# A Fourier-mixing layer with a one-token FFN: FFN weights in 128-row groups, and one ordered load list over remapped slots

## The chip, the cores and the metric

The kernel runs on one core of a Trainium2 chip. The metric is the device time of one execution in microseconds (us). Several executions were timed, and one more was profiled; all trace rows come from that one.

## The reference

A layer of 2048 tokens and 512 features with adaptive layer norm in front of two parts. `c` is one vector; six rows of 512 come from it.

```python
mod = (_silu(c) @ w_mod).reshape(1, 6, 1, -1)
sa, ca, ga, sb, cb, gb = (mod[:, i] for i in range(6))
h = _layernorm(x) * (1 + ca) + sa
a, b = h @ dft_hid_re.T, h @ dft_hid_im.T
x = x + ga * (dft_seq_re @ a - dft_seq_im @ b)          # real part of a 2-D DFT
h = _layernorm(x) * (1 + cb) + sb
r = h @ w_r                                             # one score per token
i = argmax(r)                                           # capacity 1
y = (silu(h[i] @ w_gate) * (h[i] @ w_up)) @ w_down      # F = 1792
h[i] += y * sigmoid(r[i])
x = x + gb * h
```

The DFT matrices are inputs (two of 2048x2048, two of 512x512, float32). The kernel uses their symmetry, so it must also test that the matrices it was given have it.

## The kernel before, in words

`folded` is the path that runs. `general`, a plain version, is entered only when the test of the matrices fails (`bad` > 0). Everything is float32.

**Folding.** The 16 tiles of 128 tokens (`xall`) are normalised, folded by the symmetry of the DFT in four "quads" (`quad`: `mirror`, `modulate`, `fold`, all on VectorE, then `odd_product` on TensorE), and the products of the odd class leave PSUM in `odd_exits` as `xo`. `quarter` prepares the even class, whose products and exits are in `even_sequence` (tiles `xe` and `x8`). `first(k)` handles a pair of token tiles: the hidden DFT (`hidden`, TensorE), the residual, mean and score (VectorE), the squares (ScalarE) and the deviation (GpSimd). Pairs 0 to 3 come before the even class, pairs 4 to 7 after it. `route` finds the best token; `ffn` computes its FFN in steps between which the caller puts other work; `factors(k)` (ScalarE) and `out(k)` (VectorE) make the output of pair k, and `store` writes it.

**Testing the matrices.** The two sequence matrices, sorted into 32 blocks of 128x2048 (1 MB each, "tested blocks", t0 to t31), go through the core once. `run_test` handles one: an ACTIVATE on ScalarE (line 529) that sums absolute differences, or, for the three blocks in `COUNTED`, a VectorE instruction (line 516) that counts equal elements. `test_hidden` (VectorE) and `test_hidden_sum` (ScalarE) do the hidden matrices. `verdict` sums it all up to `bad`, which every engine then loads for the branch (line 999).

**SBUF.** There are 15 slots of 1 MB (S0 to S14), some half slots (H0 to H3) and rows (`row_ca1`, ...). Every tile names its place, and a tile that takes a place waits for the readers of the tile before it.

**Loads.** Every DMA is issued by SyncE (SP) in program order, and SP waits there for the place to come free. The first loads are written out in `folded`: the token tiles (lines 849 to 851), the weights of modulation ca (852), the odd DFT blocks, the weights of sa and ga (854), small tables, hidden matrices, even blocks, then the weights of cb, sb and gb (859) into S0, S1, S2. After that come tested blocks and FFN weights in the order of `LOADS`, which also names the slot of each; a call of `load_next(n)` issues the next n of them, so that the place of the call in the program sets how far the list goes. Stores of outputs are issued by calls of `store` between them.

**FFN weights.** `w_gate` and `w_up` are each four tiles of 128 rows x 4 x 448 columns, f0 to f7. `w_down` is four tiles (f8 to f11) of FS = 112 rows x 4 x 512: `F` = 1792 is cut into 16 chunks of 112, and `load_ffn` slices the slot to `[:112]`. `project`, `columns` and `down` follow this cut.

Of the kernel before, what the change touches and what calls it, by code (L numbers as in the profile page):

```python
# [14 lines left out]
P = 128  # L15
# [8 lines left out]
FJ = F // 4  # L24
FH = FJ // 2
FS = FJ // 4
# [17 lines left out]
class Path:  # L44
# [92 lines left out]
    def mod_ca(self, t):  # L137
        nc = self.nc
        pm = self.modulation(t, "ca")
        self.ca1, self.cam = self.row("ca1"), self.row("cam")  # L140
# [4 lines left out]
    def mod_row(self, t, name, at=None, scale=1.0, bias=0.0):  # L145
        out = self.row(name, at)
        self.nc.scalar.activation(out, self.modulation(t, name), AF.Identity, scale=scale, bias=bias)
        return out


    def mod_cb(self, t):
        self.cb1 = self.mod_row(t, "cb1", scale=RD, bias=RD)

    def mod_sb(self, t):
        self.sb = self.mod_row(t, "sb", "sa")

    def mod_gb(self, t):
        self.gb = self.mod_row(t, "gb")
# [112 lines left out]
    def factor(self, j, at):  # L271
        t = self.row(f"f{j}", at)
        self.nc.scalar.activation(t, self.G, AF.Identity, scale=self.rs[:, j : j + 1], bias=1.0)  # L273
        return t
# [10 lines left out]
    def load_ffn(self, key, j, at=None):  # L285
        rows, store = (FS, self.wd) if key == "w_down" else (P, self.wg if key == "w_gate" else self.wu)
        t = self.slot(f"{key}{j}", at)[:rows, 0 : ND * FJ if rows == P else 4 * D]
        self.nc.sync.dma_start(t, self.io[key][j])
        store[j] = t.rearrange("p (k f) -> p k f", k=ND if rows == P else 4)

    def load_all_ffn(self):
        for key in ("w_gate", "w_up", "w_down"):
            for j in range(4):
                self.load_ffn(key, j)

    def route(self):
# [50 lines left out]
        tok = nc.sync.value_load(ti[0:1, 0:1], min_val=0, max_val=S - 1)  # L347
        self.row_out = self.io["out"][bass.ds(tok, 1), :]
        self.xw, self.sel, self.win, self.bst = xw, sel, win, bst
# [28 lines left out]
    def ffn(self, xs):  # L378
        nc, one = self.nc, self.one

        def project(wsb, a, name):
            dst = self.ps(name)
            for k in range(ND):
                for j in range(4):
                    nc.tensor.matmul(
                        dst[32 * j : 32 * (j + 1), :FH],
                        xs[:, k : k + 1].to_broadcast([P, 32]),
                        wsb[j][:, k, a * FH : (a + 1) * FH],
                        start=(k == 0),
                        stop=(k == ND - 1),  # L390
                        tile_position=(0, 32 * j),
                    )
            return dst[:, :FH]

        def sigmoid(pg, a):
            g = self.scrap(f"g{a}")[:, 0:FH]
# [9 lines left out]
        def columns(hf, a):  # L406
            pt = self.ps(f"pt{a}", "acc")
            for s in range(2):
                nc.tensor.matmul(
                    pt[:FS, 4 * s : 4 * s + 4],  # L410
                    hf[:, s * FS : (s + 1) * FS],
                    self.ident[:, 0:P:32],
# [3 lines left out]
            return pt  # L416

        def copied(pt, a):
            hc = one.tile([FS, 8], F32, name=f"hc{a}")
            nc.vector.tensor_copy(hc, pt[:FS, 0:8])  # L420
            return hc

        def down(hc, a, s):
            for j in range(4):
                for g in range(4):
                    nc.tensor.matmul(  # L426
                        pd[32 * g : 32 * (g + 1), 0:P],
                        hc[:, 4 * s + j : 4 * s + j + 1].to_broadcast([FS, 32]),
                        self.wd[j][:, 2 * a + s, g * P : (g + 1) * P],
                        start=(a == 0 and s == 0 and j == 0),  # L430
                        stop=(a == 1 and s == 1 and j == 3),
                        tile_position=(0, 32 * g),
                    )
# [17 lines left out]
        down(hc0, 0, 0)  # L451
        down(hc0, 0, 1)
        hc1 = copied(pt1, 1)
        down(hc1, 1, 0)
        down(hc1, 1, 1)
# [4 lines left out]
        nc.sync.dma_start(self.row_out.rearrange("o (j n) -> (o j) n", j=4), fr[0:P:32, :])  # L460
# [4 lines left out]
COUNTED = (21, 24, 27)  # L465

N_SLOTS = {(1, 0): "S3", (1, 1): "S4", (0, 0): "S5", (0, 1): "S6"}
LOADS = (
# [7 lines left out]
class Folded(Path):  # L476
    def begin(self):
        nc, const = self.nc, self.const
        self.esum = const.tile([P, NTEST + 4], F32, name="esum")
        self.cnt = const.tile([P, len(COUNTED)], F32, name="cnt")  # L480
# [4 lines left out]
        self.tests = {}  # L485
# [7 lines left out]
    def load_next(self, n=1):  # L493
        for _ in range(min(n, len(self.loads))):
            what, at = self.loads.pop(0).split(":")
            i = int(what[1:])
            if what[0] == "f":
                self.load_ffn(("w_gate", "w_up", "w_down")[i // 4], i % 4, at)
                continue
            t = self.tests[i] = self.slot(f"tst{i}", at)[:, 0:2048]  # L500
# [6 lines left out]
    def run_test(self, n=1):  # L507
        for _ in range(n):
# [17 lines left out]
            parts = [(0, 2048, i)] if i < NTEST - 1 else [(0, 1024, i), (1024, 1024, i + 1)]
            for at, w, col in parts:
# [3 lines left out]
                )  # L531

# [88 lines left out]
    def fold_cos(self, src, dst, u):  # L621
        tt = self.nc.gpsimd.tensor_tensor
# [6 lines left out]
    def lone_row(self, n):  # L629
# [84 lines left out]
    def even_sequence(self):  # L714
        nc = self.nc
        xe = self.slot("xe", "S11")[:, 0:2048].rearrange("p (a d b i s) -> p a d b i s", a=2, d=2, b=4, s=2)
        self.xe = xe.rearrange("p a d b i s -> p a d b (i s)")
        self.x8 = self.half("x8", "H3")[:, 0:1024].rearrange("p (a d b n) -> p a d b n", a=2, d=2, b=2)
# [9 lines left out]
        for part in range(2):  # L728
            for dt in range(2):
# [34 lines left out]
    def test_hidden(self):  # L764
# [4 lines left out]
        for i, t in enumerate((re, im)):  # L769
            e = self.half(f"eh{i}", f"H{i}").bitcast(BF16)[:, 0 : 3 * D].rearrange("p (k e) -> p k e", k=3)  # L770
# [26 lines left out]
    def hidden(self, j):  # L797
# [6 lines left out]
        for h in range(2):  # L804
            v = slice(h * HD, (h + 1) * HD)
            for part, w in enumerate((self.wc, sine)):
                self.nc.tensor.matmul(bank[:, v], src[:, part, h, b, :], w[:, v], start=part == 0, stop=part == 1)  # L807
        return bank

    def verdict_first(self):  # L810
# [3 lines left out]
        tot = self.tot = one.tile([P, 5], F32, name="tot")  # L814
# [3 lines left out]
        )  # L818

    def verdict_counts(self):  # L820
        nc, tot = self.nc, self.tot
        nc.vector.tensor_reduce(tot[:, 4:5], self.cnt, axis=AX.X, op=ALU.add)
        nc.vector.scalar_tensor_tensor(
            tot[:, 1:2], tot[:, 4:5], 2048.0 * len(COUNTED), tot[:, 1:2], op0=ALU.is_equal, op1=ALU.mult
# [12 lines left out]
def folded(ctx, tc, io):  # L837
# [5 lines left out]
    for zero in (p.esum, p.cnt):  # L843
        nc.gpsimd.memset(zero, 0.0)
# [14 lines left out]
    wcb, wsb, wgb = p.load_wm(4, "S0"), p.load_wm(3, "S1"), p.load_wm(5, "S2")  # L859
# [21 lines left out]

    p.shift_row(sa)
    quad(1, 0)
    p.lone_row(n[0, 0])
    p.mod_cb(wcb)
    p.mod_sb(wsb)
    p.load_next(1)
    quad(1, 1)
    p.load_next(3)
    p.run_test(3)  # L890
    p.load_next(4)
    p.mod_gb(wgb)
    quad(0, 0)
    p.load_next(2)
    p.run_test(1)
    p.load_next(1)
    p.run_test(2)
    p.turn_even()
    p.mod_b_columns()
    p.run_test(1)  # L900
    quad(0, 1)
    p.quarter(1, (z[1, 0], z[1, 1]))
    p.load_next(2)
    p.hidden_matrices(ga)
    p.hidden_turned()
    p.odd_exits()
    p.quarter(0, (z[0, 0], z[0, 1]))
    p.mod_b_router()
    p.load_next(2)
# [3 lines left out]
    fat = iter(("ca1", "cam", "f2", "gb") * 6)  # L913
# [9 lines left out]

    def factors(k):
        f[k] = [p.factor(j, next(fat)) for j in pairs[k]]

    def out(k, at=None):
# [310 lines left out]
```

## Time and profile before

| | us |
|---|---|
| runs timed | 193.48, 193.51, 189.23 (median 193.48) |
| the profiled execution, its own time | 188.67 |
| its span (first to last instruction) | 186.8 |
| busy: PE / DVE / ACT / POOL | 113.7 / 131.2 / 111.6 / 43.3 |
| the DMA queue moves | 62.97 MB, 90% of 16 engines' span |

1.9 us of the execution lie outside its span. PE is TensorE, DVE VectorE, ACT ScalarE, POOL GpSimd, SP SyncE. In the rows below times are in us from the start of the span unless marked ns; L502 is line 502 of the listing. "idle before" is how long the engine stood still before an instruction, with what released it.

### The profile page before, as it was taken

To read this page: it belongs to the slowest core of one execution; us is meant where nothing else is said; L and a number is where in the kernel's file an instruction comes from. 1 tells how busy PE (TensorE), PEld (TensorE's weight loads), DVE (VectorE), ACT (ScalarE), POOL (GpSimd) and SP (SyncE) were. 2 spreads that over 40 slices of the span, in tenths; PEclk is the share of its full clock that TensorE was granted. 3 is DMA by queue.
4 is the path that set the end of the run, shared out by engine and by line. 5 is a ranking of instruction groups with operands and counts; after the bars stand their busy time and mean duration, and the time that the engine had idled before them with its cause. 6 is when DMAs were issued, how large, how long until landed. Compare 5 with 4: busy or idle time off the path is not lost.

```text
span 186.8 us, 1976 instructions
## 1 busy us (share of the span) xinstructions
PE 113.7 (61%) x586; PEld 68.5 (37%) x586; DVE 131.2 (70%) x276; ACT 111.6 (60%) x168; POOL 43.3 (23%) x82
## 2 busy tenths in 40 slices
PE   7204997999999999999979910228922760000000
PEld 3002342343338268875658800026612650000000
DVE  1999299999999998889958860345819499990010
ACT  3074198018786586999998555519344976954500
POOL 3255519980000002229942230200000000000000
PEclk9855699999998799999999985555996675555555
DMA  5999999979999999189999999999999999999300
GB/s 160 410 431 395 404 423 392 419 318 426 420 420 430 419 418 391 56 323 382 394 414 417 221 263 237 405 282 270 235 370 402 405 359 425 414 417 413 127 11 9
DMA packets 12863, 63.17 MB, mean 338 GB/s; under 512 B 1766, under 2 KB 2795, under 8 KB 7404
## 3 DMA queue, kind: packets, MB, share of 16 engines
q1 hardware_dynamic: 12844, 62.97, 90.0%
q8 instruction: 6, 0.10, 0.2%
q14 instruction: 13, 0.11, 0.2%
HBM read 58.77 MB, written 4.20 MB: 337 GB/s over the span
## 4 chain that ended last, share of the span: by engine, by line
DMA 34%; DVE 26%; PE 20%; ACT 9%; issue 4%; SPq 2%; ACTq 0%
DMA tst<-in_tst 28%; PE h L807 8%; DMA wm<-in_wm 6%; PE so L693 6%; ACT tst L529 5%; PE pm_ca L132 3%; DVE xall L279 3%; DVE f L278 3%; DVE n L592 2%; PE pc L166 2%; SPq L122 2%; DVE p L591 2%; DVE z L604 2%; ACT f L273 1%; DVE n L586 1%
## 5 line engine op out<-in xcount | busy, mean ns | idle before, releaser
L529 ACT ACTIVATE tst<-tst,nref 128x2048 f32<-128x2048 f32 (+1 forms) x30 | 58.1, 1938 | 29.4 <-DMA tst<-in_tst 29.4
L693 PE MATMUL so<-eo,odd 128*128 128x512 f32 (+1 forms) x40 | 20.9, 653 | 1.6 <-ACT eo L557 1.4
L219 ACT ACTIVATE n<-xall,nma,rsa 128x512 f32<-128x512 f32 x16 | 11.7, 806 | 7.9 <-POOL nma L215 7.9
L255 POOL TENSOR_SCALAR rs<-ssq 128x2 f32<-128x2 f32 x8 | 1.8, 228 | 56.8 <-ACT jsq L244 56.8
L833 PE MATMUL pf<-ones,tot 128*1 128x1 f32 x2 | 0.2, 163 | 23.9 <-DVE tot L831 23.9
L229 DVE SCALAR_TENSOR_TENSOR xall<-xall,h 128x512 f32<-128x512 f32 x16 | 11.0, 685 | 4.7 <-PE h L807 4.7
L807 PE MATMUL h<-whid,xo 128*128 128x256 f32 x64 | 14.1, 381 | 0.0
L244 ACT ACTIVATE jsq<-xall,mean 128x512 bf16<-128x512 f32 x16 | 11.5, 716 | 3.4 <-DVE mean L237 3.2
L807 PEld LDWEIGHTS h<-whid,xo 128*128 128x128 f32 x64 | 12.1, 190 | 2.4 <-ACT xo L712 0.8
L132 PE MATMUL pm_ca<-wm,sc 128*128 128x512 f32 x8 | 6.4, 967 | 10.8 <-DMA wm<-in_wm 10.8
L261 DVE SCALAR_TENSOR_TENSOR tv<-xall,mean,vr 128x512 bf16<-128x512 f32 x16 | 12.0, 752 | 0.6
L273 ACT ACTIVATE f<-cb,rs 128x512 f32<-128x512 f32 x16 | 10.7, 711 | 2.7 <-DVE xall L279 2.7
L278 DVE SCALAR_TENSOR_TENSOR f<-xall,mean,f 128x512 f32<-128x512 f32 x16 | 11.9, 747 | 0.3 <-ACT f L273 0.3
L208 DVE BATCH_NORM_STATS2 st<-xall 128x6 f32<-128x512 f32 x16 | 10.6, 662 | 2.1 <-DMA xall<-in_x 2.1
L807 PE MATMUL h<-whid,xe 128*128 128x256 f32 x48 | 11.1, 381 | 1.3 <-ACT xe L738 1.3
L693 PEld LDWEIGHTS so<-eo,odd 128*128 128x128 f32 (+1 forms) x40 | 6.3, 181 | 15.1 <-issue 11.4
L279 DVE SCALAR_TENSOR_TENSOR xall<-sb,mean,f 128x512 f32<-128x512 f32 x14 | 10.5, 752 | 0.5
L807 PEld LDWEIGHTS h<-whid,xe 128*128 128x128 f32 x48 | 9.0, 190 | 2.9 <-ACT xe L738 1.7
L516 DVE TENSOR_SCALAR_CACHE_REDUCE tst<-tst,nref 128x2048 bf16<-128x2048 f32 x3 | 7.0, 2344 | 3.8 <-DMA tst<-in_tst 3.8
L833 PEld LDWEIGHTS pf<-ones,tot 128*1 128x1 f32 x2 | 0.1, 80 | 24.3 <-issue 24.3
L426 PE MATMUL pd<-w_down,hc 112*32 112x128 f32 x128 | 6.8, 397 | 2.7 <-DVE hc L420 2.7
L591 DVE TENSOR_TENSOR p<-p,ca 128x1024 f32<-128x1024 f32 x4 | 5.9, 1486 | 3.5 <-ACT ca L141 3.5
(199 smaller groups left out, 244.8 us busy)
## 6 DMA issues: line engine op xcount, KB each, us to landing
tst<-in_tst SPq DMA_DIRECT2D x31, 1024.0 KB, 11.2
wm<-in_wm SPq DMA_DIRECT2D x6, 1024.0 KB, 11.3
xall<-in_x SPq DMA_DIRECT2D x8, 512.0 KB, 5.7
w_gate<-in_w_gate SPq DMA_DIRECT2D x4, 896.0 KB, 6.0
w_up<-in_w_up SPq DMA_DIRECT2D x4, 896.0 KB, 8.2
w_down<-in_w_down SPq DMA_DIRECT2D x4, 896.0 KB, 20.1
out<-xall SPq DMA_DIRECT2D x7, 512.0 KB, 11.8
wt<-in_wt SPq DMA_DIRECT2D x2, 1024.0 KB, 9.6
```

The source lines that it names most:

```text
L132: self.nc.tensor.matmul(dst, self.sc[:, k : k + 1].to_broadcast([P, P]), t[:, k, :], start=(k == 0), stop=(k == ND - 1))
L208: nc.vector.bn_stats(st[:, 6 * i : 6 * i + 6], src)
L219: self.nc.scalar.activation(dst.rearrange("p (b r j) -> p r b j", b=4, r=2), src.rearrange("p (r b j) -> p r b j", b=4, r=2), AF.Identity, ...
L229: self.nc.vector.scalar_tensor_tensor(x, x, 1.0, y, op0=ALU.mult, op1=ALU.add, accum_out=self.sums[:, j : j + 1])
L244: self.nc.scalar.activation(junk, self.xall[:, j, :], AF.Square, bias=self.mean[:, j : j + 1], accum_out=self.ssq[:, j : j + 1],)
L261: self.nc.vector.scalar_tensor_tensor(junk, self.xall[:, j, :], self.mean[:, j : j + 1], self.vr, op0=ALU.add, op1=ALU.mult, accum_out=sel ...
L273: self.nc.scalar.activation(t, self.G, AF.Identity, scale=self.rs[:, j : j + 1], bias=1.0)
L278: nc.vector.scalar_tensor_tensor(t, x, mean, t, op0=ALU.add, op1=ALU.mult)
L279: nc.vector.scalar_tensor_tensor(dst, self.sg, mean, t, op0=ALU.subtract, op1=ALU.add)
L529: self.nc.scalar.activation(v, v, AF.Abs, bias=self.nref[:, col : col + 1], accum_out=self.esum[:, col : col + 1])
L693: self.nc.tensor.matmul(dst, a, b, start=first and i == 0, stop=last and i == len(ops) - 1)
L807: self.nc.tensor.matmul(bank[:, v], src[:, part, h, b, :], w[:, v], start=part == 0, stop=part == 1)
```

## The change

- **FFN in groups of 128 rows.** `F` is cut into NG = 7 groups of 256 columns. `w_gate` and `w_up` are packed into one input `w_in` of seven tiles of 128x2048; `w_down` becomes 128 rows x 14 chunks x 512, loaded as three tiles of 4 chunks and one of 2 (f7 to f10). All loads of weights now fill 128 partitions. `project` runs four groups, then three; `down` uses 14 chunks of 128 rows.
- **One ordered list.** `load_next` is gone. `free(names)` marks slots as free and issues everything at the head of `LOADS` whose slot is free; `run_test` frees its own slot. The list now also holds the weights of cb, sb, gb (m4, m3, m5) and the stores (o0 to o7). It never skips an entry.
- **Slots.** Tested blocks turn over in S0 to S3 for most of the list; `xo` moves from S6 to S11, `xe` to H0 and H1, and some rows share places.
- **Order.** The weights of ca are loaded ahead of the second half of the tokens. The modulations cb, sb, gb go between the quads, each after one, and the first tests among them; `shift_row` moves from POOL to DVE and behind the second quad; `mod_b_columns` moves behind `first(3)`; `factors(0)` and `out(0)` move behind the whole even sequence, with `test_hidden_sum` behind them. All 32 tests run on ACT (`COUNTED` and `verdict_counts` are gone); 13 tests stand ahead of the second half of the pairs, 3 among it, 16 after `route`.

The core of the diff:

```diff
-FJ = F // 4
-FH = FJ // 2
-FS = FJ // 4
+FG = 2 * P
+NG = F // FG
...
-COUNTED = (21, 24, 27)
 LOADS = (
-    "t0:S3 t1:S4 t2:S0 t3:S1 t4:S3 f0:S7 t5:S4 t6:S0 t7:S5 t8:S2 t9:S1"
-    " f1:S13 t10:S3 f2:S14 t11:S4 f3:S1 t12:S0 t13:S5 f4:S4 t14:S2 f5:S3 t15:S0"
-    " f6:S6 t16:S5 f9:S9 t17:S2 f10:S10 t18:S0 f7:S8 t19:S5 f8:S12 t20:S2 f11:S11 t21:S0"
-    " t22:S5 t23:S2 t24:S0 t25:S7 t26:S13 t27:S14 t28:S1 t29:S4 t30:S3 t31:S6"
+    "t0:S0 t1:S1 t2:S3 m4:S2 t3:S4 m3:S7 m5:S5 t4:S0 t5:S1 t6:S3 t7:S2 f0:S7 t8:S4 f1:S6 t9:S0"
+    " f2:S13 f3:S5 t10:S1 f4:S14 t11:S3 f5:S4 t12:S2 f6:S11 t13:S0 f7:S9 t14:S1 f8:S10 t15:S3"
+    " f9:S8 t16:S2 f10:S12 o0 t17:S0 t18:S1 t19:S3 t20:S2 t21:S0 t22:S1 t23:S3 o1 t24:S2 t25:S0"
+    " o2 t26:S7 t27:S6 o3 t28:S13 t29:S5 o4 t30:S14 o5 t31:S4 o6 o7"
 ).split()
...
+    def free(self, *names):
+        self.taken -= set(names)
+        while self.loads:
+            what, _, at = self.loads[0].partition(":")
+            i = int(what[1:])
+            if at in self.taken or (what[0] == "o" and i not in self.outs):
+                return
+            self.loads.pop(0)
+            self.taken.add(at)
+            self.taken.discard("")
+            if what[0] == "o":
+                self.store(*self.outs[i])
+                continue
+            if what[0] == "m":
+                self.wmod[i] = self.load_wm(i, at)
+                continue
+            if what[0] == "f":
+                self.load_ffn(i, at, self.last if i == 10 else None)
+                continue
+            self.home[i] = at
...
-    for cls in (1, 0):
-        for i in (0, 2, 1, 3):
-            p.load_x(cls, i)
+    for i in (0, 2, 1, 3):
+        p.load_x(1, i)
     wca = p.load_wm(1, "S0")
+    for i in (0, 2, 1, 3):
+        p.load_x(0, i)
...
-    wcb, wsb, wgb = p.load_wm(4, "S0"), p.load_wm(3, "S1"), p.load_wm(5, "S2")
...
+    quad(1, 0)
+    p.free("S0", "S1", "S2", "S3")
+    p.lone_row(n[0, 0])
+    quad(1, 1)
+    p.free("S4", "S7")
     p.shift_row(sa)
...
+    pcb = p.modulation(p.wmod[4], "cb")
+    p.free("S2")
     p.run_test(3)
     quad(0, 0)
+    p.free("S5")
     p.run_test(1)
+    p.exit_cb(pcb)
+    psb = p.modulation(p.wmod[3], "sb")
+    p.exit_sb(psb)
+    p.free("S7")
     p.run_test(1)
     quad(0, 1)
+    pgb = p.modulation(p.wmod[5], "gb")
+    p.free("S5", "S6")
+    p.run_test(1)
...
     for k in range(4):
         first(k)
+        if k < 3:
+            p.run_test(1)
+    p.free("S11")
+    p.mod_b_columns()
     p.mod_b_products()
     p.mod_b_corners()
     p.test_hidden()
     p.test_hidden_rest()
+    p.free("S9", "S10")
     for i, _ in enumerate(p.even_sequence()):
-        if i == 0:
-            factors(0)
-        else:
+        if i:
             p.run_test(1)
+    factors(0)
+    p.last = p.slot("last", "S12")
+    p.free("S8", "S12")
+    out(0, p.last[:, 2 * D : 4 * D].rearrange("p (i e) -> p i e", i=2))
+    p.test_hidden_sum()
     for k in range(4, 8):
         first(k)
         if k < 7:
             p.run_test(1)
     xs = p.route()
-    p.run_test(2)
+    p.run_test(3)
     steps = p.ffn(xs)
     factors(1)
+    p.run_test(1)
     factors(2)
+    p.run_test(1)
     next(steps)
     out(1)
     p.run_test(1)
     next(steps)
+    p.free(*gates)
     factors(3)
     out(2)
     p.run_test(2)
...
-        "w_down": f["B_w_down"][:, fx].reshape(4, 4, FS, D).transpose(0, 2, 1, 3).reshape(4, FS, 4 * D),
+        "w_in": w_in,
+        "w_down": f["B_w_down"][:, fx].reshape(2 * NG, P, D).transpose(1, 0, 2).reshape(P, -1),
```

## Rows read from the trace of the kernel before

**Rows 1.** The page: bytes a second in 40 slices of 4.7 us, and the queue

```profile
GB/s 160 410 431 395 404 423 392 419 318 426 420 420 430 419 418 391 56 323 382 394 414 417 221 263 237 405 282 270 235 370 402 405 359 425 414 417 413 127 11 9
...
q1 hardware_dynamic: 12844, 62.97, 90.0%
```

**Rows 2.** Windows: busy PE, PEld, DVE, ACT, POOL, PE clock, DMA share, GB/s

```profile
42.50:75.00 32.50, 32.30 (x94) 17.49 (x94) 30.93 (x60) 23.86 (x32) 1.16 (x3) 0.95 1.01 418
75.00:82.50 7.50, 7.50 (x37) 6.56 (x35) 6.55 (x20) 7.44 (x15) 2.28 (x6) 1.00 0.38 139
...
102.50:117.50 15.00, 5.82 (x27) 4.77 (x26) 7.40 (x22) 8.52 (x16) 2.61 (x6) 0.77 1.02 247
...
122.50:137.50 15.00, 10.76 (x142) 7.21 (x142) 8.78 (x28) 8.27 (x12) 0.00 (x0) 0.71 1.01 255
137.50:175.00 37.50, 8.02 (x140) 6.85 (x140) 24.30 (x40) 22.91 (x29) 0.00 (x0) 0.60 0.99 398
```

**Rows 3.** Tile views: w_gate's landings, then w_down's issues (ns, first and last start) and landings

```profile
DMA to landing us min/median/max: 4.5/6.0/7.6
...
L288 SPq DMA_DIRECT2D w_down<-in_w_down x4: 363/402/424, 95.4 to 116.7; - x4
...
DMA to landing us min/median/max: 14.6/20.1/21.3
```

**Rows 4.** Timeline of SP at the gap: start, duration of the issue

```profile
68.62 0.38 SPq L502 DMA_DIRECT2D tst<-in_tst  x1
78.93 0.33 SPq L288 DMA_DIRECT2D w_gate<-in_w_gate  x1
```

**Rows 5.** The chain that ended last, near its start: start, duration, what

```profile
5.09 11.26 DMA wm<-in_wm
...
16.49 6.37 PE pm_ca L132 x8
```

**Rows 6.** Timeline of DVE: start, duration, instruction, idle before it

```profile
18.83 1.22 DVE L586 TENSOR_TENSOR n<-n 128x1024 f32<-128x1024 f32 x1
...
31.52 2.33 DVE L586 TENSOR_TENSOR n<-n 128x1024 f32<-128x1024 f32 x1
...
69.82 0.68 DVE L229 SCALAR_TENSOR_TENSOR xall<-xall,h 128x512 f32<-128x512 f32 x1
...
96.27 0.69 DVE L229 SCALAR_TENSOR_TENSOR xall<-xall,h 128x512 f32<-128x512 f32 x1 [1.25 <-PE h L807]
...
118.94 0.17 DVE L299 TENSOR_TENSOR r<-r,rs 128x16 f32<-128x16 f32 x1 [8.09 <-POOL rs L256]
...
128.18 0.16 DVE L346 TENSOR_TENSOR xs<-xs,cbs 128x4 f32<-128x4 f32 x1
```

**Rows 7.** Timeline of PE: start, duration, instructions

```profile
42.63 4.74 PE L693 MATMUL so<-eo,odd 128*128 128x512 f32 x10
...
55.78 2.02 PE L166 MATMUL pc<-ones,cb 1*128 1x1 f32 x8
...
67.03 14.08 PE L807 MATMUL h<-whid,xo 128*128 128x256 f32 x64
...
91.86 1.03 PE L693 MATMUL sz<-ee,eve 128*128 128x258 f32 x4
```

**Rows 8.** ACT: the group of tests (page), then its timeline

```profile
L529 ACT ACTIVATE tst<-tst,nref 128x2048 f32<-128x2048 f32 (+1 forms) x30 | 58.1, 1938 | 29.4 <-DMA tst<-in_tst 29.4
...
75.28 0.70 ACT L244 ACTIVATE jsq<-xall,mean 128x512 bf16<-128x512 f32 x1
...
78.81 0.71 ACT L244 ACTIVATE jsq<-xall,mean 128x512 bf16<-128x512 f32 x1
...
128.38 2.55 ACT L273 ACTIVATE f<-cb,rs 128x512 f32<-128x512 f32 x4
```

**Rows 9.** The chain at its end: start, duration, what

```profile
165.30 9.59 DMA tst<-in_tst
...
178.21 0.14 DVE bad L834
```

More of the change, by code (lines that the diff above doesn't have):

```diff
@@ L283, in store, with load_ffn @@
         self.nc.sync.dma_start(self.some(out, tiles), o)
[L285 to L289, printed above, removed]
+    def load_ffn(self, i, at=None, tile=None):
+        t = self.slot(f"ffn{i}", at) if tile is None else tile
+        if i < 10:
+            t = t[:, 0 : 4 * D]
+        else:
+            t = t[:, 0 : 2 * D]
+        key, i = ("w_in", i) if i < 7 else ("w_down", i - 7)
+        src = self.io[key]
+        if key == "w_in":
+            self.nc.sync.dma_start(t, src[i])
+            t = t.rearrange("p (g k f) -> p g k f", g=2, k=ND)
+            for h in range(2):
+                (self.wu if (h if i == 6 else i > 2) else self.wg)[6 if i == 6 else 2 * (i % 3) + h] = t[:, h]
+        else:
+            n = t.shape[1] // D
+            self.nc.sync.dma_start(t, src[:, 4 * D * i : 4 * D * i + n * D])
+            for h in range(n):
+                self.wd[4 * i + h] = t[:, h * D : (h + 1) * D]
     def load_all_ffn(self):
-        for key in ("w_gate", "w_up", "w_down"):
-            for j in range(4):
-                self.load_ffn(key, j)
+        for i in range(11):
+            self.load_ffn(i)
     def route(self):
@@ L484, in begin @@
         self.lrow = const.tile([1, ZC], F32, name="lrow")
-        self.tests = {}
+        self.tests, self.home, self.wmod, self.outs = {}, {}, {}, {}
+        self.taken = {f"S{i}" for i in range(15)}
         self.loads, self.next_run = list(LOADS), 0
@@ L842, in folded @@
     p.keep_warm(16)
-    for zero in (p.esum, p.cnt):
-        nc.gpsimd.memset(zero, 0.0)
+    nc.gpsimd.memset(p.esum, 0.0)
     w = p.const.tile([P, 3, D], F32, name="whid")
@@ L922, in first, with spot, out @@
         p.deviations(pairs[k])
-    def factors(k):
-        f[k] = [p.factor(j, next(fat)) for j in pairs[k]]
-    def out(k, at=None):
-        if at is not None:
-            o[k] = p.half(f"o{k}", at)[:, 0 : 2 * D].rearrange("p (i e) -> p i e", i=2)
-        else:
-            o[k] = p.some(p.xall, pairs[k])
+    spots = ("cab0", "cab1", "f2", "gb")
+    turn = []
+    def spot(j):
+        at = spots[len(turn) % 4]
+        turn.append(at)
+        return p.row(f"f{j}", at) if at[:3] != "cab" else p.fab[:, int(at[3]), :]
+    def factors(k):
+        f[k] = [p.factor(j, spot(j)) for j in pairs[k]]
+    def out(k, dst=None):
+        dst = p.some(p.xall, pairs[k]) if dst is None else dst
         for i, j in enumerate(pairs[k]):
-            p.output(j, f[k][i], o[k][:, i, :])
+            p.output(j, f[k][i], dst[:, i, :])
+        p.outs[k] = pairs[k], dst
+        p.free()
     for k in range(4):
-        p.run_test(1)
-        p.load_next(2)
         first(k)
-    p.run_test(1)
-    p.load_next(2)
+        if k < 3:
+            p.run_test(1)
+    p.free("S11")
+    p.mod_b_columns()
     p.mod_b_products()
@@ L990, in folded @@
         p.run_test(1)
-        p.load_next(k == 4)
-        p.store(pairs[k], o[k])
-    p.load_next(len(p.loads))
     next(steps, None)
-    p.run_test(NTEST - 1 - p.next_run)
-    p.verdict_counts()
-    p.run_test(1)
+    p.run_test(NTEST)
     p.verdict()
@@ L1179, in _layouts @@
     flat = tok.reshape(NT, P)
+    group = lambda w: w[fx].reshape(P, ND, NG, FG).transpose(2, 0, 1, 3).reshape(NG, P, ND * FG)
+    wg, wu = group(f["B_w_gate"]), group(f["B_w_up"])
+    both_of = lambda a, b: np.concatenate([a, b], axis=1)
+    w_in = np.stack(
+        [both_of(w[2 * i], w[2 * i + 1]) for w in (wg, wu) for i in range(3)] + [both_of(wg[6], wu[6])]
+    )
     feeds = {
```

205 lines of the change are left out of this document (85 added, 120 removed).

## The prediction

> **What bounds the kernel now.** I read the page's rate of the DMA queue first: it stands near 420 GB/s in most slices, so the stream of 62.97 MB is the first suspect [rows 1]. At the 418 GB/s of an undisturbed stretch [rows 2] it would take 150.6 us. The stream starts at about 2.5 us (the first slice's 160 GB/s says so) and its last load lands at 165.30 + 9.59 = 174.9 [rows 9], so some 22 us went elsewhere. The windows show where. In two stretches of 15 us the engines of the queue are fully busy (share 1.02 and 1.01) but move only 247 and 255 GB/s [rows 2]: 7.53 MB, which at 418 take 18.0 us, so 12.0 are lost. From 75 to 82.5 the queue is idle for the most part (share 0.38, 139 GB/s): 1.04 MB, worth 2.5 us, so 5.0 are lost. SP's timeline gives the cause: after the issue at 68.62 the next comes at 78.93, because the head of the list waits for its slot [rows 4]. 2.5 + 150.6 + 12.0 + 5.0 = 170.1; the 4.8 left lie in small stretches, such as the 398 GB/s of the last window [rows 2]. Behind the stream come the last test, the verdict (`bad` done at 178.35 [rows 9]) and 8.45 us of branch and leave-taking up to the span's end at 186.8.
>
> The second chain is the computing. It sets where slots come free, and it waits for the stream in turn: ACT stands 29.4 us in all before tests for landings [rows 8], and DVE 8.09 before route [rows 6].
>
> **The change, part by part.**
>
> *112 rows.* The w_down tiles take 20.1 us from issue to landing where w_gate tiles of the same bytes take 6.0 [rows 3], they are issued from 95.4 to 116.7 [rows 3], and with such landings they are on their way in the two slow stretches, where the other engines are less busy than elsewhere [rows 2]. Their four tiles of 0.92 MB are the only loads of that weight that leave partitions out. I take the whole 12.0 us as gone; the bounds are 0 (the new form at the old 250) and 12.0. The weights in 128 rows otherwise move the same bytes, so w_in at 418 costs what w_gate and w_up do.
>
> The port rule of the Trainium skill ("SBUF — State Buffer", Door 1: The DMA port swizzle) ties the rate to how many of 16 ports the partitions reach, and by its table 112 partitions still reach all of them; the page "DMA: Bandwidth & Descriptors" (Why a DMA increments its semaphore by 16 and not by 1) has such a load spread over all 16 engines. By these two nothing would be lost by the shape, and the stream would stay 12.0 longer than I take it to; the rows above show a loss while these tiles move, so I follow the rows. No row here shows the ports themselves.
>
> *Early order.* The load of ca lands at 5.09 + 11.26 = 16.35 [rows 5]; four loads of 0.52 MB now go behind it, 2.1 MB or 5.0 us, so 11.3. Its matmuls (6.37 us [rows 5]) end at 17.7 instead of 22.9. The gain is capped: DVE's statistics and first mirror end at 20.05 [rows 6], about 1.2 later now because the second half of the tokens lands 2.5 later. DVE's chain starts modulating at 21.2 instead of 23.5 (22.9 and ACT's exit), less 0.4 for a POOL memset queued behind statistics. shift_row on DVE costs at most 1.5 (its 512 columns are half of the 1.22 us row), and takes its share of POOL's disturbance away (the same mirror step takes 2.33 beside POOL's work, 1.22 without [rows 6]; most of that is the lone row, which stays). The second quad ends some 3.0 earlier, the fourth some 1.7.
>
> *PE's order.* The 16 tiny matmuls of pc (twice 2.0 us [rows 7]) leave their place before the last odd product, and pm_sb and pm_gb (eight matmuls each, 3.8 by the 4.74 for ten [rows 7]) stand between and behind the products. PE is busy from the third product on in both orders, so the hidden products still start near 67 [rows 7]; the first residual comes at 68.8 for 69.82 [rows 6].
>
> *A new wait at S7.* m3 needs S7, that is the second odd product's end: 42.63 - 3.0 + 4.74 = 44.4 [rows 7]. Ahead of it lie 10.5 + 5 MiB, which run out at 2.5 + 38.9 and about 1.2 for the tiny loads: 42.6. A load into an empty queue lands 4.5 us after issue at best [rows 3], of which 2.2 are its 0.92 MB; the lead of 2.3 makes the gap 4.1. Queued behind m3 on SP are m5 and t4 to t7; who waits is psb on PE, which has the third product to do first. From here on I find each slot free before its turn: the list stays full to f10, at about 110.
>
> *The even class.* pc now stands behind the hidden products: 81.1 + 3.9 = 85.0. The even sequence lasts 92.9 - 81.1 = 11.8 [rows 7], so PE ends it at 96.8. ACT then has the third group's exits (its products end 1.8 earlier, two times about 0.9), t11, the last exits, t12 and factors(0) in its queue; four small exits I put at 1.4, below the 1.55 of a pair of squares: 95.0 + 1.4 + 2.0 + 1.4 + 2.0 + 1.2 = 103.0. out(0) is on DVE ahead of first(4), which therefore starts at about 105.5, not at 96.27 [rows 6]: 9 us late. What pays for it: in the kernel before, waits for landings follow here, and they go.
>
> *Second half of the pairs.* ACT needs 78.81 - 75.28 = 3.53 us for a pair with a test [rows 8], DVE some 3.2, so ACT paces it: 105.5 + 1.7 + 3 x 3.53 + 1.55 = 119.3 for the last squares, route at 120.4 (118.94 before [rows 6]), the token ready 128.34 - 118.94 = 9.4 later, at 129.8.
>
> *ACT from there.* Three tests come from DVE; at 58.1 us for 30 instructions [rows 8], with the read of the sum, a whole test costs 1.98, so 5.9 more; DVE is relieved off the path. Behind route stand 15 tests (29.7), the last in halves (2.5), 14 factors at 2.55/4 = 0.64 [rows 8] (8.9), small activations (0.7) and two waits for the gate products (about 1.5 each, since ACT is through its earlier tests 1.5 before pg0 ends): 119.3 + 44.8 = 164.1.
>
> *The stream from f10.* t17 waits for t13's test (gap about 1.5), t18 to t20 each for a test at ACT's pace (3.53 less 2.5 for 1 MiB: three gaps of 1.0), then three tests in a row refill it. o1 waits for out(1) at 133.5 and holds what is behind it; with the lead the bytes start at 135.8. From there o1 to o7 and t24 to t31, 12.06 MB (eight of 1.05, seven of 0.52), go at the 398 GB/s that a stretch with stores shows [rows 2]: 30.3, to 166.1. Check by the sum: 2.5 + 150.6 + 4.1 + 4.5 + 2.5 = 164.2, up to 169 with the 4.8 of small losses.
>
> *The end.* o6 and o7 now stand behind t31: t31's bytes end 2.6 before 166.1, land near 164.5, and `bad` is done near 166.7. The row's store waits for o7 (167.1), takes 0.7 to issue, and SP reads `bad` behind it: 167.9 + 8.45 = 176.3. With the 1.9 outside the span that is 178 us, against 188.67 for the profiled execution, whose own sum this is. The median of the runs shown is 193.48, 2.5% above it; a median of runs after may stand above 178 by as much.
>
> 256 instead of 224 columns a matmul, and 112 for 128 in `down`, change PE by under a microsecond beside waits of ACT, and are put at nothing; without that cover they would cost under 1.
>
> **The rivals.** *A: the forecast, 172 to 184.* For it: rate and landings [rows 2, 3]; against it: a chain of many slot times, each good to 1 or 2 us.
>
> *B: the slots come free early enough.* If out(0) does not hold first(4) (ACT finds t11 and t12 done beside PE) and o1 comes in time, route is at 113, ACT ends at 157, and the stream at 2.5 + 150.6 + 4.8 = 157.9: 170 us. For it: PE's idle share is small up to here, and each of my ACT steps is an upper bound. Against: the program order of ACT, in which three tests stand ahead of factors(0).
>
> *C: 112 rows are not the cause.* Something else of those weights or stretches stays slow, +12.0 between 94 and 110. The gaps behind it (4.5, and part of o1's) are then filled by the late stream, so 6.5 remain: 184.5. For it: tested blocks in these stretches are slow too. Against: landings of 20.1 for w_down alone [rows 3].
>
> *D: slower, by the turn of the slots.* From t17 to t25 a load goes out only after the test four places ahead. If ACT is kept so far that just one landed block waits at a time, a turn costs 4.8 (issue to landing) + 1.98 instead of the 2.5 to 3.5 counted, 3.8 more each; from four such turns on the kernel is no faster than before (193), all nine give 212; I put it at 196. For it: the list never skips, and ACT does factors and waits for PE between. Against: four blocks are 7.9 us of testing, longer than one turn.
>
> *E: small shortfalls together, 184 to 190*, among them PE at the lower of its two clocks (1.2 GHz), which the granted 0.60 to 0.77 of three windows holds in part [rows 2]: the products after a pause would take up to twice as long.
>
> **How the numbers follow.** A 0.60, B 0.14, C 0.10, D 0.06, E 0.10. The likeliest is A, 178. The range runs from below B, 168, to above C and E, 190, and leaves out most of D and the edge of B. A measurement of this kernel can tell about 2% from no change. Faster by more: A, B and the better part of C and E, 0.82; within 2%: 0.12; slower: D, 0.06.
>
> **What would show it.** Right: no stretch at 250 GB/s with a full share; w_down landings as the others'; a gap near 43 to 47; first(4) near 105; route near 120; stores last. Wrong: slow stretches with the new tiles (C); ACT waiting for landings behind route (D); first(4) before 100 (B).

## The result, and the profile of the changed kernel

The changed kernel takes 180.53 us (median of four runs, 180.01 to 181.12) against 192.63 for the kernel before (189.23 to 193.51): 0.9477 of its time, 95% interval 0.9356 to 0.9598. Some executions come out more than 1.5% above the fastest of the same kernel; the medians are of all runs, while ratios, and the differences given for the last four kernels below, leave those executions out. The profiled execution took 180.28 us with a span of 178.5 (before: 188.67 and 186.8). Forecast: 178 us.

The page, against [rows 1] and the first line of [rows 8]: the rate in 40 slices of 4.5 us, the queue, the group of tests on ACT with the idle time in front of them, and the loads of `w_down` (count, size, median time from issue to landing).

```profile
GB/s 164 383 410 396 428 394 399 420 419 240 29 433 419 433 419 422 417 420 428 419 419 417 419 426 417 354 305 257 393 334 331 335 406 313 434 417 410 256 13 7
...
q1 hardware_dynamic: 12764, 62.97, 89.4%
...
L545 ACT ACTIVATE tst<-tst,nref 128x2048 f32<-128x2048 f32 (+1 forms) x33 | 64.0, 1941 | 4.2 <-DVE n L600 2.8
...
ffn<-in_w_down SPq DMA_DIRECT2D x3, 1024.0 KB, 9.3
```

The same 62.97 MB flow, but the dips to 221 to 282 GB/s in the middle of [rows 1] are gone; a new hole (240, 29) stands near 45 us, and from 112 to 152 us the rate is down to 257 to 406. ACT stood 29.4 us before tests for landings; now 4.2 us in all, of which landings explain 1.2. The full tiles of `w_down` land in 9.3 us where those of 112 rows took 20.1 [rows 3].

The windows, against [rows 2] (busy PE, PEld, DVE, ACT, POOL, then PE clock, DMA share, GB/s):

```profile
42.50:50.00 7.50, 7.50 (x15) 2.36 (x14) 7.29 (x12) 2.10 (x2) 0.00 (x0) 0.83 0.29 83
50.00:75.00 25.00, 24.85 (x73) 12.46 (x72) 22.32 (x46) 13.43 (x22) 0.51 (x2) 1.00 1.01 423
75.00:82.50 7.50, 7.50 (x36) 6.39 (x34) 6.42 (x19) 7.43 (x13) 2.73 (x7) 1.00 1.02 423
82.50:102.50 20.00, 19.25 (x73) 13.39 (x73) 10.78 (x23) 12.62 (x28) 9.83 (x17) 0.91 1.01 420
102.50:117.50 15.00, 11.70 (x53) 9.63 (x52) 12.66 (x34) 13.91 (x24) 2.52 (x6) 1.00 0.98 387
117.50:137.50 20.00, 9.84 (x72) 5.86 (x76) 9.40 (x38) 18.00 (x24) 2.79 (x6) 0.57 0.91 333
137.50:150.00 12.50, 7.44 (x140) 4.89 (x132) 7.89 (x16) 10.45 (x16) 0.00 (x0) 1.00 0.99 343
150.00:170.00 20.00, 2.98 (x50) 2.28 (x50) 13.10 (x25) 17.17 (x21) 0.00 (x0) 0.61 0.91 367
```

No stretch shows a full share with 250 GB/s any more: 75 to 82.5 went from 139 to 423, and 102.5 to 117.5 from 247 to 387. In exchange, ACT is now busy in 18.00 of 20 us and 17.17 of 20 us of the late stretches.

SP's timeline shows the new hole, against [rows 4]: m3 (the first `wm`) goes out 9.0 us after the issue before it.

```profile
38.15 0.33 SPq L530 DMA_DIRECT2D tst<-in_tst  x1
47.16 0.95 SPq L125 DMA_DIRECT2D wm<-in_wm  x2
```

PE's timeline, against [rows 7]: the second odd product, pc, the first and the last part of the even sequence.

```profile
40.60 6.50 PE L710 MATMUL so<-eo,odd 128*128 128x512 f32 x10 [2.43 <-DVE odd L625]
...
67.95 14.08 PE L830 MATMUL h<-whid,xo 128*128 128x256 f32 x64
...
81.96 2.02 PE L168 MATMUL pc<-ones,cb 1*128 1x1 f32 x8
...
85.78 1.84 PE L710 MATMUL st<-ee,eve 128*128 128x256 f32 x4
87.42 1.92 PE L710 MATMUL sz<-ee,eve 128*128 128x258 f32 x4
...
98.07 1.03 PE L710 MATMUL sz<-ee,eve 128*128 128x258 f32 x4
```

The same four `sz` matmuls take 1.92 us behind pc and 1.03 at the end of the sequence, as in [rows 7]; the same ten `so` matmuls 6.50 behind an idle time of 2.43, where [rows 7] has 4.74. That is PE at its lower clock: the granted clock is 0.66 from 40.6 to 44.0 us and 0.54 from 85.75 to 89.25, where 0.5 is the lower level (1.2 GHz), and 1.00 from 78 to 85.75, pc included. The kernel before shows it, too, at its third odd product, which there stands behind pc; a line of PE's timeline, and a window by the columns above:

```profile
59.60 6.45 PE L693 MATMUL so<-eo,odd 128*128 128x512 f32 x10
...
60.00:63.00 3.00, 3.00 (x4) 0.78 (x3) 2.86 (x8) 2.51 (x5) 0.00 (x0) 0.52 1.03 431
```

DVE's timeline, against [rows 6]: out(0) with the wait in front of it, the first residual of the second half, route, and the end of `bad`.

```profile
104.38 0.75 DVE L279 SCALAR_TENSOR_TENSOR f<-xall,mean,f 128x512 f32<-128x512 f32 x1 [9.60 <-ACT f L274]
...
107.35 0.68 DVE L231 SCALAR_TENSOR_TENSOR xall<-xall,h 128x512 f32<-128x512 f32 x1
...
122.31 0.17 DVE L312 TENSOR_TENSOR r<-r,rs 128x16 f32<-128x16 f32 x1 [2.83 <-POOL rs L258]
...
169.33 0.15 DVE L850 TENSOR_SCALAR bad<-pf 1x1 int32<-1x1 f32 x1 [0.37 <-PE pf L849]
```

First(4) starts at 107.35 instead of 96.27, and yet `bad` comes 8.9 us earlier than in [rows 9]: what used to follow, the waits for landings, is gone.

ACT's timeline from factors(0) to the last test:

```profile
103.64 1.33 ACT L274 ACTIVATE f<-cb,rs 128x512 f32<-128x512 f32 x2
...
135.51 0.39 ACT L409 ACTIVATE g<-pg 128x256 f32<-128x256 f32 x1 [1.96 <-PE pg L397]
...
139.93 0.38 ACT L409 ACTIVATE g<-pg 96x256 f32<-96x256 f32 x1 [2.05 <-PE pg L397]
...
166.09 1.15 ACT L545 ACTIVATE tst<-tst,nref 128x1024 f32<-128x1024 f32 x1 [0.42 <-DMA tst<-in_tst]
```

From the last squares (121.17) to the last test's end (168.5) ACT stands still only for 5.4 us, of which a landing explains 0.42. The chain that ended last shows the same. Its shares of the span by engine, before and after:

```profile
DMA 34%; DVE 26%; PE 20%; ACT 9%; issue 4%; SPq 2%; ACTq 0%
```

```profile
DVE 32%; PE 29%; ACT 14%; DMA 10%; issue 5%; POOL 3%; SPq 2%; DVEq 0%; ACTq 0%; POOLq 0%
```

Loads were its largest part and are now a tenth of the span. Near its end stands the last load, t31, as in [rows 9]:

```profile
155.90 0.76 DVE xall L280
156.68 0.40 SPq L284
...
157.17 8.84 DMA tst<-in_tst
...
166.09 2.46 ACT tst L545 x4
```

t31 goes out behind the store o5, which waits for out(5) on DVE. Its slot S4 had been free since 142.24, when the last product with the weights in it ended; but the list never skips. Over the whole run SP waits 26.7 us for tests to give slots back, and 16.4 us for the outputs of stores.

By this chain the bound has moved from the stream to the order of the program on PE, ACT and DVE, which the list passes on to the last load. The experiments on the list, on pc and on the two tests bear on it.

### The profile page after: what moved, and what is told of

The parts are those of the page before. It is cut to its first block, busy times and chain, and to the rows that moved or that the text cites. A ratio compares the mean times of both kernels' runs of the same rounds, so it can differ in the third digit from the quotient of the medians.

```text
span 178.5 us, 1918 instructions
## 1 busy us (share of the span) xinstructions
PE 118.5 (66%) x554; PEld 68.2 (38%) x554; DVE 124.8 (70%) x273; ACT 117.9 (66%) x174; POOL 36.9 (21%) x76
## 3 DMA queue, kind: packets, MB, share of 16 engines
q1 hardware_dynamic: 12764, 62.97, 89.4%
## 4 chain that ended last, share of the span: by engine, by line
DVE 32%; PE 29%; ACT 14%; DMA 10%; issue 5%; POOL 3%; SPq 2%; DVEq 0%; ACTq 0%; POOLq 0%
ACT tst L545 8%; PE h L830 8%; DMA xall<-in_x 5%; DMA tst<-in_tst 5%; PE sz L710 4%; ACT jsq L246 3%; DVE n L609 3%; PE pg L397 3%; PE st L710 3%; PE so L710 3%; DVE st L210 3%; PE pc L168 2%; DVE uv L617 2%; PE pm_gb L131 2%; DVE p L608 2%
## 5 line engine op out<-in xcount | busy, mean ns | idle before, releaser
L545 ACT ACTIVATE tst<-tst,nref 128x2048 f32<-128x2048 f32 (+1 forms) x33 | 64.0, 1941 | 4.2 <-DVE n L600 2.8
L279 DVE SCALAR_TENSOR_TENSOR f<-xall,mean,f 128x512 f32<-128x512 f32 x8 | 6.0, 745 | 9.6 <-ACT f L274 9.6
L131 PE MATMUL pm_sa<-wm,sc 128*128 128x512 f32 x8 | 6.5, 988 | 3.8 <-DMA wm<-in_wm 3.8
L443 PE MATMUL pd<-ffn,hc 128*32 128x128 f32 x96 | 4.1, 322 | 5.4 <-DVE hc L434 5.4
L131 PEld LDWEIGHTS pm_ca<-wm,sc 128*128 128x128 f32 x8 | 2.5, 330 | 10.2 <-DVE mv L211 7.1
L258 POOL TENSOR_TENSOR rs<-rs,nhalf 128x2 f32<-128x2 f32 x8 | 6.2, 779 | 0.7
L710 PE MATMUL st<-ee,eve 128*128 128x256 f32 (+1 forms) x20 | 6.3, 441 | 0.0
L609 DVE TENSOR_TENSOR n<-n,cab 128x1024 f32<-128x1024 f32 x4 | 5.9, 1484 | 0.5 <-POOL cab L143 0.5
```

The lines of the kernel that those rows point to most:

```text
L131: self.nc.tensor.matmul(dst, self.sc[:, k : k + 1].to_broadcast([P, P]), t[:, k, :], start=(k == 0), stop=(k == ND - 1))
L258: nc.gpsimd.tensor_tensor(rs, rs, self.nhalf[:, 0 : len(tiles)], op=ALU.pow)
L279: nc.vector.scalar_tensor_tensor(t, x, mean, t, op0=ALU.add, op1=ALU.mult)
L545: self.nc.scalar.activation(v, v, AF.Abs, bias=self.nref[:, col : col + 1], accum_out=self.esum[:, col : col + 1])
L609: self.nc.vector.tensor_tensor(pm[1], pm[1], row(self.cam), op=ALU.mult)
L710: self.nc.tensor.matmul(dst, a, b, start=first and i == 0, stop=last and i == len(ops) - 1)
```

## The experiments

The theory: the loads of 112 rows cost most of the time, whatever they carry. Its rivals: something else about those stretches (C); the hole at S7 belongs to the sum (the forecast's own step); or the program order around the even sequence sets the end. The first four kernels ran beside one another, with the kernel before at 190.99 us (189.08 to 192.9) and without the changed kernel, whose figures are those of the result; the last four ran together, on another chip, with the kernel before at 191.81 (189.07 to 196.1).

### The kernel before with `w_down` padded to 128 rows

```diff
-        t = self.slot(f"{key}{j}", at)[:rows, ...]
+        t = self.slot(f"{key}{j}", at)[:, ...]
...
+        t = t[:rows]
...
+        "w_down": np.pad(..., ((0, 0), (0, P - FS), (0, 0))),
```

> The kernel before, with one thing changed: each w_down tile is padded with 16 rows of zeros, so that its load fills 128 partitions instead of 112 (0.52 MB more in all). Theory, 112 rows are the cause of the slow stretches: both stretches at 250 GB/s go, the w_down tiles land within some 6 to 12 us of their issue like the tested blocks instead of 20, 12.0 us less 1.3 for the added bytes come off the stream, and ScalarE's waits for landings before route with them: 177 to 181 us in a run like the one profiled (188.67), a ratio near 0.95, most of the whole gain by this alone. Rival C, the cause lies elsewhere in those weights or stretches: the stretches stay at 250 GB/s and the time is 1 us longer, 189 to 192.

Measured: 181.38 us (180.45 to 183.29), 0.9498 of the kernel before (0.9402 to 0.9594). Its windows, by the columns above, and the landings of `w_down`:

```profile
75.00:82.50 7.50, 7.50 (x36) 6.62 (x35) 6.55 (x21) 7.43 (x13) 2.48 (x8) 1.00 0.34 111
102.50:117.50 15.00, 7.55 (x36) 5.71 (x34) 9.65 (x33) 11.41 (x20) 3.44 (x10) 0.79 1.01 425
122.50:137.50 15.00, 11.58 (x160) 7.45 (x164) 11.99 (x23) 10.15 (x15) 0.00 (x0) 0.73 0.89 324
137.50:175.00 37.50, 5.83 (x126) 4.77 (x118) 19.94 (x36) 20.19 (x25) 0.00 (x0) 0.55 0.81 318
```

```profile
DMA to landing us min/median/max: 11.2/13.7/14.5
```

More bytes (0.52 MB) arrive sooner: from 102.5 to 117.5 us 425 GB/s move instead of 247, and w_down lands in 13.7 instead of 20.1 [rows 3] (6 to 12 were expected). Rival C falls. This edit alone gives nearly all that the whole change gives. Route comes at 114.39, 8 us before that of the changed kernel; but the old idle stretch (111 GB/s from 75 to 82.5) and a thin queue at the end (share 0.81) stay, and ACT still waits 17.8 us for landings.

### The changed kernel with its `w_down` loads cut into 112 + 16 rows

```diff
-            self.nc.sync.dma_start(t, src[:, ...])
+            for r in (slice(0, 112), slice(112, P)):
+                self.nc.sync.dma_start(t[r], src[r, ...])
```

> The changed kernel, with the loads f7 to f10 of w_down cut in two along the partitions, 112 and 16 rows; same bytes, four more DMAs. Theory, 112 rows are the cause: the rate falls to 250 GB/s while they move (about 94 to 120 us), the stream is 8 to 12 us late at t17, the idle stretches behind it (about 4.5 us of waiting for tests, and part of that before o1) take up some of that: 183 to 187 us, ratio to the kernel before 0.97 to 0.99. Rival C: no stretch at 250, 180 to 181.5 as without the cut.

Measured: 184.17 us (183.17 to 186.06), 0.9681 (0.9599 to 0.9764). Its windows:

```profile
92.50:102.50 10.00, 9.25 (x39) 5.74 (x40) 2.11 (x4) 8.37 (x16) 2.39 (x6) 1.00 1.03 292
102.50:117.50 15.00, 11.54 (x53) 9.49 (x51) 12.83 (x35) 13.86 (x24) 2.53 (x6) 1.00 1.02 246
```

The slow stretch is back at its old height, 246 GB/s at a share of 1.02. Against the changed kernel's 420 and 387 GB/s, 10 x (1 - 292/420) + 15 x (1 - 246/387) = 3.0 + 5.5 = 8.5 us of stream are lost here, and ACT now waits 13.4 us for landings. The span rises by 2.9 only (181.4 for 178.5): route is hardly later (122.68 for 122.31), and the stream makes up for some of it behind (372 GB/s from 117.5 to 137.5, for 333). That is within what was expected, 183 to 187.

### The same cut on four tested blocks (t10 to t13), nothing done to the weights

```diff
-            if i < NTEST - 1:
+            if 10 <= i < 14:
+                for r in (slice(0, 112), slice(112, P)):
+                    self.nc.sync.dma_start(t[r], self.io["tst"][i][r])
+            elif i < NTEST - 1:
```

> The changed kernel, with the loads of four tested blocks, t10 to t13, cut into 112 and 16 rows; nothing about w_down is changed. They move between about 72 and 93 us, where the changed kernel holds 420 GB/s. Theory, the number of partitions is the cause whatever is loaded: the rate falls to about 250 GB/s in that stretch, some 15 us long, and these blocks land late by up to 10 us. Rival C, it is a matter of those weights (their place in HBM or their row length): the stretch stays at 420 GB/s. The time as such tells less, 181 to 190.

Measured, one run: 184.74 us (its own time; the changed kernel's profiled execution 180.28). Its windows:

```profile
50.00:65.00 15.00, 14.90 (x34) 5.43 (x33) 14.52 (x27) 7.54 (x13) 0.00 (x0) 1.00 1.01 424
...
75.00:95.00 20.00, 20.00 (x79) 14.98 (x78) 16.58 (x41) 14.19 (x30) 11.89 (x21) 0.91 1.02 301
95.00:102.50 7.50, 6.75 (x30) 5.01 (x29) 0.00 (x0) 4.54 (x11) 0.00 (x0) 1.00 1.03 246
```

The slow stretch follows the shape to another tensor, another slot and another time, and ACT stands 15.1 us before tests for landings (1.2 in the changed kernel). It is the 112 rows, not the weights. (The pieces of 16 rows may have a part in it here and in the run above; the kernel before had none, and the same rate.) By the Trainium skill ("DMA: Bandwidth & Descriptors", Why a DMA increments its semaphore by 16 and not by 1) a load of 112 rows is spread over all 16 engines, since 16 divides 112. The full share (1.01 to 1.03) agrees with that; the rate of 246 shows that this is not enough. Which part of the path is slow no run here tells.

### The hole at S7 closed by reordering the list

```diff
-    "... m4:S2 t3:S4 m3:S7 m5:S5 t4:S0 t5:S1 t6:S3 t7:S2 ..."
+    "... m4:S2 t3:S4 t4:S0 t5:S1 t6:S3 m3:S7 m5:S5 t7:S2 ..."
```

> The changed kernel with three entries of the list moved: t4, t5 and t6 ahead of m3 and m5, so that SP does not stand at S7 while their slots are free. The idle stretch of the queue from about 43 to 48 us should go in either theory. Theory of the prediction's second chain, ScalarE's program order sets the end from the even class on: the blocks land 4 to 6 us earlier, but their tests stand where they stood, and the time is the same to within 1 us, 179.5 to 181. Rival, the sum of the stream sets the end: the 5 us of idle come off, 175 to 177.

Measured: 182.09 us (180.89 to 184.35), 0.9523 (0.9425 to 0.962). Its windows:

```profile
42.50:50.00 7.50, 7.50 (x14) 2.24 (x13) 7.29 (x12) 2.10 (x2) 0.00 (x0) 0.80 1.01 423
50.00:75.00 25.00, 24.86 (x72) 12.38 (x71) 22.44 (x46) 13.29 (x22) 0.40 (x2) 1.00 0.92 378
...
82.50:102.50 20.00, 19.66 (x67) 13.27 (x67) 10.90 (x23) 11.02 (x25) 9.93 (x17) 0.83 0.85 338
```

The hole is filled (423 for 83 GB/s; 7.5 x (1 - 83/423) = 6.0 us of stream), and the time is no shorter: the same bytes are missing later (378 and 338 GB/s), since slots come free no earlier (f0 goes out at 58.71, for 58.57 in the changed kernel). The 175 to 177 of the rival are out; at 182.09 the time is even above the 179.5 to 181 of the theory. First(4) comes at 109.11 for 107.35. Of these 1.8 us, 1.6 are the even sequence, 14.8 us for 13.2, at a granted clock of 0.83 for 0.91. Less that, the time is that of the changed kernel: six microseconds of idle queue cost nothing measurable here.

### The changed kernel again, and factors(0) ahead of the first tests

The first is the changed kernel as it is, for comparison on this chip:

> The changed kernel as it is, beside the next three on one chip. Both theories: 180 to 181.5 us.

Measured: 181.57 us (178.83 to 182.8), 0.9413 (0.9282 to 0.9544). The second:

```diff
+    turn += [0, 0]
...
         if i:
             p.run_test(1)
+        else:
+            factors(0)
...
-    turn += [0, 0]
-    factors(0)
```

> The changed kernel with factors(0) at its old place, behind the first group of exits of the even class; out(0) stays behind the sequence. Theory, program order on ScalarE and VectorE sets the end from the even class on: out(0) no longer waits behind three tests, the first residual of the second half comes near 102.5 instead of 107.4, but ScalarE then does test_hidden_sum until about 106.7 where its first squares now start at 108.9, so route and the end come 2 us earlier: 178 to 179 us. Rival, landings set the end: no change, 180 to 181.5.

Measured: 179.11 us (177.09 to 179.98), 0.9364 (0.9264 to 0.9464). It is 1.2 us below the changed kernel beside it (178.18 against 179.38), and the intervals overlap for the most part: a gain of this edit alone is not settled. In its profiled execution (179.98 us) first(4) comes at 104.40, where 102.5 was expected, and the first squares of the second half start at 109.08, for 108.89 in the changed kernel: ACT, which has `test_hidden_sum` in front of them, is done with it only then; PE's granted clock from 82.5 to 102.5 is 0.74 there, for 0.91.

### pc left out

```diff
-    p.mod_b_columns()
+    nc.gpsimd.memset(p.cbs, 0.0)
```

> The changed kernel with the sixteen small matmuls of mod_b_columns and their copy left out (the two rows that they turn are zero, so the one routed token's FFN gets another input; all other work is the same). It prices the move of these matmuls to between the hidden products and the even class. Theory of program order: PE reaches the even class 3.9 us earlier, and a clock that stays at its upper level may give 1.5 more; everything behind moves with it, 175 to 177 us. Rival, landings set the end: 180 to 181.5.

Measured: 174.19 us (172.78 to 176.25), 0.9141 (0.9051 to 0.9231), below the 175 to 177 expected. Against the changed kernel beside it that is 5.45 us less (173.93 against 179.38), and every run is below that kernel's fastest. PE's timeline behind the hidden products, then DVE's at first(4) and at `bad`:

```profile
81.14 1.03 PE L710 MATMUL st<-ee,eve 128*128 128x256 f32 x4
82.00 1.03 PE L710 MATMUL sz<-ee,eve 128*128 128x258 f32 x4
```

```profile
100.96 0.68 DVE L231 SCALAR_TENSOR_TENSOR xall<-xall,h 128x512 f32<-128x512 f32 x1
...
162.83 0.14 DVE L850 TENSOR_SCALAR bad<-pf 1x1 int32<-1x1 f32 x1 [0.37 <-PE pf L849]
```

Without the 16 tiny matmuls the even sequence starts at 81.14 and its first eight matmuls take 1.03 a group for 1.84 and 1.92: 4.6 us earlier at the start (85.78), 6.4 at first(4), 6.5 at `bad`. Of the 4.6, pc itself is 3.8 and 0.7 lies ahead of the edit (the hidden products start at 67.22 for 67.95); the 1.8 that come on top up to first(4) are the matmuls behind pc. The clock granted from 85.75 to 89.25 is 1.00 here and 0.54 with pc. What stands here on PE goes to the end almost one for one.

### Two tests moved to DVE's idle time, factors(0) first

```diff
+COUNTED = (10, 11)
...
+            if i in COUNTED:
...
+                self.nc.vector.tensor_scalar(
...
+                    op0=ALU.is_equal,
+                    op1=ALU.add,
...
+    turn += [0, 0]
+    p.run_test(2)
...
-        if i:
+        if i == 0:
+            factors(0)
+        elif i == 1:
+            p.test_hidden_sum()
+        elif i == 3:
             p.run_test(1)
...
-    turn += [0, 0]
-    factors(0)
...
-    p.test_hidden_sum()
```

The two blocks t10 and t11 are counted on DVE, by the form of instruction that the kernel before had at line 516, ahead of the even sequence.

> The changed kernel with t10 and t11 counted on VectorE (which stands idle for 9.6 us before out(0)), factors(0) behind the first group of exits, test_hidden_sum behind the second, and t12 behind the last. Theory of program order: the first squares of the second half start near 104.2 instead of 108.9, and route and the end come up to 4.7 us earlier, less what the stream then sets: 175.5 to 178 us, faster than both kernels. Rival, landings set the end: 180 to 181.5.

Measured: 176.2 us (174.29 to 179.3), 0.9237 (0.9128 to 0.9345). Its windows, and DVE's timeline:

```profile
82.50:102.50 20.00, 20.00 (x78) 14.34 (x78) 18.43 (x31) 13.48 (x31) 9.62 (x15) 0.91 1.01 415
102.50:117.50 15.00, 10.26 (x48) 8.47 (x46) 11.87 (x38) 14.13 (x24) 4.54 (x12) 0.96 1.01 401
117.50:137.50 20.00, 14.62 (x159) 9.13 (x162) 12.25 (x39) 17.01 (x21) 0.00 (x0) 0.69 1.01 405
137.50:150.00 12.50, 4.33 (x106) 3.44 (x96) 8.89 (x18) 11.55 (x16) 0.00 (x0) 0.86 1.01 402
```

```profile
101.65 0.68 DVE L231 SCALAR_TENSOR_TENSOR xall<-xall,h 128x512 f32<-128x512 f32 x1
...
163.05 0.14 DVE L870 TENSOR_SCALAR bad<-pf 1x1 int32<-1x1 f32 x1 [0.37 <-PE pf L869]
```

DVE's 9.60 us of waiting at out(0) now hold two tests (18.43 us busy for 10.78 from 82.5 to 102.5), first(4) comes 5.7 earlier, and the stream stays above 400 GB/s to 150 us, since what the list waits for comes sooner (t17 goes out at 106.85 for 112.57, o5 at 150.21 for 156.68). `bad` is 6.3 earlier. The time is within the 175.5 to 178 expected. This version beats both kernels: against the changed kernel beside it by 4.1 us (175.30 against 179.38), and all its runs but one are below that kernel's fastest. How much of it each of the moves gives is not shown. Moving pc behind the last residual as well was not tried.

## Why the prediction was right, and where it was off

Right were the direction, the cause and the size: 178 us, and 180.28 for the profiled execution, 180.53 in the median. The miss is 2.3 us, in sizes that partly cancel; that it came out so small is in part luck.

- *112 rows, 12.0 us of stream.* Right, and shown from three sides: taking them from the kernel before gains 9.6 us (a ratio of 0.9498), putting such loads back costs 2.9 of the span, and tested blocks show the same. That the rest of the change then adds little (0.9498 alone; 0.9477 and 0.9413 for the whole, in other sets of runs) I did not foresee. The parts do not add: with the cut loads put back the others still stand at 0.9681. Both remedies seem to go at one loss, ACT's waits for landings: 29.4 us before, 17.8 with the padding, 13.4 with the rest, and 1.2 with both. That is read from the four traces; no run isolates it.
- *The gap of 75 to 82.5 goes.* Right: 423 GB/s.
- *The early order.* Near: modulate starts at 22.00 for 21.2, the hidden products at 67.95 for 67, the first residual at 69.98 for 68.8.
- *The wait at S7.* The hole is there, but its size was wrong: "42.63 - 3.0 + 4.74 = 44.4" took the second odd product at 4.74 us. Behind 2.43 us of PE's idle time it ran 6.50, ended near 47, and m3 went out at 47.16 instead of 44.4. That the gap belongs in the sum over the stream was wrong too: closing it left the time where it was. The stream had slack there.
- *The even class: "so PE ends it at 96.8".* This is the step that failed, as a mis-sized term: "The even sequence lasts 11.8" came from [rows 7], where it follows dense matmuls. Behind the 16 tiny matmuls its first groups took 1.84 and 1.92 for 1.03, and the hidden products behind it started at 98.95: 13.2 us instead of 11.8, and 0.8 came in from before. The kernel before pays the same price at its third odd product, 6.45 for 4.74. The forecast moved the 3.9 us of pc and not the 1.7 behind them. In the changed kernel factors(0) and first(4) were then 1.9 late (107.35 for 105.5), and route (122.31 for 120.4) and the token (131.56 for 129.8) by the same. ACT's pace of 3.53 us a pair held: squares at 108.89, 112.45, 115.99 and 119.53.
- *ACT from there, 44.8 us.* It took 47.4, to 168.5 for 164.1. Tests and factors were right; the waits were too small: 4.0 for the two gate products for 3.0, and 1.4 that I had not counted.
- *The stream from f10.* "the list stays full to f10" held until about 112. Then the rate fell further than counted (333, 343 and 367 GB/s for 398). Up to 131 that is slots that came free late. From 135 on it is the stores: the forecast let all of o1 to o7 and t24 to t31 flow behind o1, but o2 to o5 each held the list until DVE had their output (o2 at 141.54, o3 at 145.66, o4 at 153.78, o5 at 156.68). This was the stream's answer to ACT and DVE, not the bound: in the last version, where both are earlier, it runs at 401 to 405.
- *The end.* `bad` at 169.48 for 166.7. Of the 2.8 us, the landing of t31 is 1.5 (166.0 for 164.5). The other 1.3 are a slip in the sum: it allows 2.2 us from that landing to `bad`, where [rows 9] has 3.46 (174.89 to 178.35) and the changed kernel took 3.47. The row's store behind it was issued by 170.77, and 7.73 us remain, where I had 8.45.

Of the rivals, C fell to the padded kernel. B missed its condition: out(0) does hold first(4), by 9.60 us of waiting on DVE. D did not come: ACT waits for landings only 0.42 us behind route. E's lower clock came in two places, behind a pause at 40.6 and behind pc without a pause, and is most of the 1.9.

## What to carry to other kernels

Load all 128 partitions, with padding if need be: 14% more bytes in a tile were cheaper here than a tile of 112 rows (the one other count that was measured), which slows its neighbours in the queue as well. When a stream stops being the bound, its holes stop costing, as the hole at S7 did here; read then which engine gives the slots back, and what stands ahead of that in its program order. A store in an ordered list of loads holds every load behind it until its output is done. A few tiny matmuls between dense ones cost their own time and then the lower clock of those behind them (here 3.9 us and some 1.7), so put them where that engine has slack.

## What the hardware showed that was not expected

- Loads of 112 rows, or of 112 + 16, hold the queue's engines at a share of 1.01 to 1.03 while 246 to 255 GB/s move, against 418 to 425 with 128 rows: in four stretches of three kernels, on two kinds of tensor.
- A queue that is refilled one load at a time shows a high share and a low rate, too: 0.91 and 333 GB/s from 117.5 to 137.5, where SP waits for a test before nearly every load. A high share alone does not say that the stream is at its limit.
- PE's granted clock from 82.5 to 102.5 us is 0.91 with pc at the head of the even sequence and 1.00 without it, although PE has hardly any idle time there (19.25 of 20 us busy). Right behind the 16 matmuls of 1x1, which count as 3.9 us of busy time, it is 0.54 (85.75 to 89.25); in the kernel before, behind the same 16 at another place, 0.52 (60 to 63).
